# Raw FFN weights loaded ahead of the second batch's v, one weight conversion moved into the attention, and named places for x and the last h

## The chip, the core and the metric

The kernel runs on one core of one Trainium2 chip. A core has a matrix engine (TensorE, in the rows PE, with its weight loads as PEld), three elementwise engines (VectorE as DVE, ScalarE as ACT, GpSimd as POOL) and a sync engine (SP) that here issues nearly all transfers. Each engine works its own list of instructions in order; semaphores join them. The metric is the device time of one execution in microseconds.

## The reference

What is computed, cut to what matters here:

```python
# attention, B=2, H=8, S=576, D=64: two parts that are added
#  q, k and v averaged over groups of 4 -> softmax attention on 144 positions, repeated 4 times
#  plus attention in which a position sees only those less than 4 away
x = attn_out                                  # 1152 tokens x 512
h = x @ w_in; g = relu(h) + log1p(exp(-|h|))  # w_in 512 x 2048
x = g @ w_out                                 # w_out 2048 x 512
P = exp(x @ w_gate - max)                     # 8 experts, then 8 rounds of row and column norms
out = sum over e of P[:, e] * (relu(x @ w1[e]) @ w2[e])
```

The FFN's weights come as 64-bit floats and the answer is wanted in 32-bit accuracy.

## The kernel before

There are three stages, and the order of every engine's list is fixed before the run by a scheduler that follows the order of the code, the waits and a timeline of its own.

**Attention** (to about 121 us). `emit` walks 36 units: 16 pooled ones (`pooled`, tiles named with a d: pd, ptd, pvd, pxd) and 20 local ones (`local`, with an l: pl, ptl, pvl, pxl), batch 0 first. A unit has four steps on PE: scores (pd or pl), transposes (pt), values (pv), and a transpose back (px). Step k of a unit is written two units behind step k-1, so four units are under way at once. DVE takes the maximum (nm) and normalises, ACT does the exponentials (e) and copies the transposes (ptls, ptds, upT), DVE adds both parts into xf, and GpSimd splits xf into a rounded part and the rest in x. There are three x tiles of 384 tokens, x0 to x2. `fill` and `warm` add products of zeros.

The v of batch 1 for the pooled part comes by `load_vd(1)`: two transfers vr of 640 KB, which GpSimd adds up into vs and then vd. Its vs tiles use the same buffers (tags "ch" and "cs", one of each) as the weight conversion below. The local part's v comes by small transfers vw.

**FFN** (to about 305 us). Four blocks of 512 of the 2048 middle columns, for each three chunks of 384 tokens: `l1` (products ph, line 471, then softplus on ACT and DVE into h) and `l2` (products py, line 513, added into yp). Each block needs four weight tiles of two halves, made by `prep(n)`, n = 0 to 15: `load_raw` brings 1 MB of 64-bit numbers (raw, two buffers), and `from_double` turns them into w with three ACT and seven DVE instructions (lines 133 to 146; in the first four the last of the seven runs on GpSimd). `prep(n)` also loads raw n+2. The first block's conversions and its first products are placed among the attention units by the table `at`; `prep(4)` and all later ones are called in the FFN loop, after the first, second or third `l1` of a block.

**Experts** (to the end). Products pu (line 564) and po (line 613) with weights prepared from 32-bit numbers.

The SP queue holds its transfers in the order of the code: k and q of batch 1, then vr twice, then raw 0 and raw 1, then vw, and further raw between the vw. A transfer whose buffer is not free stops all behind it.

Places: the three x tiles, the two vr tiles of batch 1 and later s0 shared a pool of three turning buffers (`xyp`, tag "xy"). The last h of the FFN had a pool of its own (`late`). The weight tiles turn over six places, four in `wp` and two in `wp2`, and `wp2` is opened only when the attention's pools are closed.

Of the kernel before, what the change touches and what calls it, by code (L numbers as in the profile page):

```python
# [8 lines left out]
F32 = mybir.dt.float32  # L9
F32R = mybir.dt.float32r  # L10
# [11 lines left out]
P = 128  # L22
# [10 lines left out]
CH = 384  # L33
NCH = NT // CH
KD = DM // P
FB = 512
NFT = FB // P
NFB = FF // FB
# [5 lines left out]
WIN = [min(max(HQ * t - POOLF + 1, 0), S - KW) for t in range(2 * NQT)]  # L44
OFF = [tuple(HQ * t - WIN[t] for t in (2 * u, 2 * u + 1)) for u in range(NQT)]
KINDS = sorted(set(OFF))
NRING = 6
EARLY = 4
PAIR = CH // 2
# [31 lines left out]
class Net:  # L81
# [66 lines left out]
    def prep(self, n):  # L148
        if n >= 4 * NFB:
            return  # L150
        self.load_raw(n)
        i = n % NRING
        pool = self.wp if i < EARLY else self.wp2
        w = pool.tile([P, 2, 1024], F32R, tag=f"w{i}", name=f"w{n}")
        self.from_double(n, w)
        self.load_raw(n + 2)
        self.ws[n] = w
# [128 lines left out]
    def load_vd(self, b):  # L286
        nc = self.nc
        vd = self.atp.tile([GH, 2, H, DA], F32, tag="vd", name=f"vd{b}", bufs=2)
        nc.gpsimd.memset(vd[:, :, :, D:DA], 1.0)
        for hf in range(2):  # L290
            pool, tag = (self.rawp, "raw") if b == 0 else (self.xyp, "xy")
            r = pool.tile([GP, POOLF, DM], F32, tag=tag, name=f"vr{b}{hf}")
            nc.sync.dma_start(out=r, in_=self.a["vp"][b, hf].rearrange("p (f d) -> p f d", f=POOLF))
            s = self.convp.tile([GH, 2, DM], F32, tag=("ch", "cs")[hf], name=f"vs{b}{hf}", bufs=1)
            e = nc.vector if b == 0 else nc.gpsimd
            e.tensor_tensor(s, r[:GH, 0:2], r[:GH, 2:4], ALU.add)
            sv = s.rearrange("p f (h d) -> p f h d", h=H)
            e.tensor_tensor(vd[:, hf, :, 0:D], sv[:, 0], sv[:, 1], ALU.add)
        self.vd[b] = vd
        self.upT[b] = self.atp.tile([P, NPAIR, G], F32, tag="upT", name=f"upT{b}", bufs=2)  # L300
# [65 lines left out]
    def local(self, b, t, g):  # L366
# [56 lines left out]
        def s4():  # L423
# [16 lines left out]
            while n < nq:  # L440
                c, o = divmod(tok + n, CH)
                m = min(nq - n, CH - o)
                if c not in self.x:
                    self.x[c] = self.xyp.tile([P, 2, KD, CH], F32R, tag="xy", name=f"x{c}")
                hi, lo = (self.x[c][:, i, 2 * g : 2 * g + 2, o : o + m] for i in range(2))
                nc.gpsimd.tensor_copy(hi, xf[:, :, n : n + m])
                nc.gpsimd.tensor_tensor(lo, xf[:, :, n : n + m], split(hi), ALU.subtract)
                n += m
# [44 lines left out]
        self.made = (act.ins, dve.ins)  # L493

    def l1(self, blk, c, nf=2):
        pool, tag = (self.late, "h") if (blk, c) == (NFB - 1, NCH - 1) else (self.hp, "h")
        h = pool.tile([P, 2, NFT, CH], F32R, tag=tag, name=f"h{blk}_{c}")
        self.h[blk, c] = h
        return [lambda f=f: self.l1_unit(blk, c, f, nf, h) for f in range(0, NFT, nf)]
# [242 lines left out]
    def run(self):  # L742
        stack = ExitStack()
        xstack = ExitStack()
        self.xyp = xstack.enter_context(self.tc.tile_pool(name="xyp", bufs=NCH))
        self.attention_pools(stack)
        self.h, self.ypart, self.acc, self.wa, self.T = {}, {}, {}, {}, {}
        self.x = {}
# [46 lines left out]
                self.load_qk(1, p)  # L795

        def load_rest():
            self.load_vd(1)
            self.load_raw(1)

        def prep(n, lag):

# [6 lines left out]
        at = {1: [load_second], 9: [load_rest]}  # L809
        for p in range(NPAIR):  # L810
            at.setdefault(11 + p, []).append(lambda p=p: self.pool_qk(1, p))
        for n, lag, u in zip(range(2 * NFT), (1, 1, 0, 0), (16, 19, 23, 29)):
            at.setdefault(u, []).append(lambda n=n, lag=lag: prep(n, lag))
        one, two, after = self.l1(0, 0, 1), self.l2(0, 0, 1), self.l1(0, 1, 1)
        for m, u in zip(one + two[:2], (22, 24, 26, 28, 30, 32)):
            at.setdefault(u, []).append(m)
        at[36] = [after[0], after[1], two[2], after[2], after[3], two[3]]
# [15 lines left out]
        def opened(name, to=self.ctx, **kw):  # L833
            return to.enter_context(self.tc.tile_pool(name=name, reuse_waits="tile", **kw))

        def edge(name, to=self.ctx):
            opened(name, to, bufs=1, side="right").tile([P, EDGE], F32, name=name)
# [34 lines left out]
        for b, c in items[: -NCH + 1]:  # L872
            first_product(b, c)
            if c == 1:
                self.prep(4 * (b + 1) + 1)
            if c == 2:
                self.prep(4 * (b + 1) + 2)
            if pending not in (None, (0, 0)):
                second_product(*pending)
            if c == 0:  # L880
                self.prep(4 * (b + 1))
            if c == 2:
                self.prep(4 * (b + 1) + 3)
            pending = (b, c)

        b = NFB - 1
        wstack.close()
        self.ap = opened("ap", bufs=1, side="right")
        edge("edge2")
        self.late = opened("late", bufs=1, side="right")  # L890

        s0 = self.xyp.tile([P, 2, 4, 2, P], F32, tag="xy", name="s0")
        parts = [(0, i, *part) for i in range(2) for part in self.sums_up(0, i, s0[:, i])]
        first_product(b, 1)
        first_product(b, 2)
        turn_over()
        for n in (1, 3, 0):
            self.behind(lambda: self.part_up(*parts[n]))
        second_product(b, 0)
# [128 lines left out]
```

## Time and profile before

| | us |
|---|---|
| runs of the kernel before, median of 3 | 1057.45 |
| lowest and highest of them | 1054.2 and 1062.04 |
| the profiled execution, its own time | 1064.65 |
| span of the profiled execution | 1062.9 |
| instructions | 16399 |

The span is what the trace shows between the first and the last instruction; the profiled execution's own time is 1.75 us more. The profile lists for each engine what it did and what it waited for, and for PE the clock that the chip granted it: 1.00 is its upper level, 2.4 GHz, and 0.50 its lower, 1.2 GHz. PE is counted busy for 1050.3 of the 1062.9 us, but a product at the lower clock counts as busy too, for longer.

### The profile page before, as it was taken

What the parts mean: (1) busy time and instruction counts of PE and PEld (TensorE: products, weight loads), DVE (VectorE), ACT (ScalarE), POOL (GpSimd) and SP (SyncE); (2) the same over time, 40 slices, a digit from 0 to 9 for tenths busy, and PEclk for the clock granted to TensorE, in tenths of its full rate; (3) what the DMA queues carried; (4) which work ended last, traced back from release to release, by engine and by line L of the source; (5) the groups of instructions that cost most, each with busy time, mean ns of one, the idle gap of its engine ahead of it and who ended that gap; (6) DMA issues with size and microseconds to landing.
All of it is one profiled execution on the core that took longest, in us unless ns stands there. A gap on an engine that the chain in (4) does not pass through costs nothing.

```text
span 1062.9 us, 16399 instructions
## 1 busy us (share of the span) xinstructions
PE 1050.3 (99%) x6570; PEld 945.1 (89%) x6570; DVE 775.2 (73%) x1470; ACT 428.7 (40%) x815; POOL 162.5 (15%) x210
## 2 busy tenths in 40 slices
PE   8999999999999999999999999999999999999998
PEld 5667999999998899898989989898998989899897
DVE  6578699999987687784947658494765848576572
ACT  5567697776743433241413324141331414133130
POOL 2653300002112220111202011120201112020000
PEclk9789999999999999999999999999999999999999
DMA  9532032222111221111211111121111112110003
GB/s 286 167 97 75 2 119 80 80 80 80 40 40 40 80 80 40 40 41 40 80 40 41 40 40 40 40 81 40 40 40 41 41 40 80 41 40 1 1 2 89
DMA packets 14348, 63.92 MB, mean 60 GB/s; under 512 B 1792, under 2 KB 4608, under 8 KB 7808
## 3 DMA queue, kind: packets, MB, share of 16 engines
q1 hardware_dynamic: 13696, 61.70, 17.9%
q8 instruction: 51, 0.84, 0.3%
q10 hardware_dynamic: 576, 1.18, 0.3%
q14 instruction: 25, 0.20, 0.1%
HBM read 60.51 MB, written 2.36 MB: 59 GB/s over the span
## 4 chain that ended last, share of the span: by engine, by line
PE 89%; DVE 5%; DMA 3%; ACT 2%; issue 1%; SPq 0%; DVEq 0%; ACTq 0%
PE po L613 37%; PE pu L564 33%; PE ph L471 7%; PE py L513 6%; DMA raw<-in_w 1%; DMA k<-in_k 1%; PE pvl L406 1%; PE pl L385 1%; DMA vw<-in_vw 1%; DVE h L492 1%; PE pxl L426 1%; DVE r L488 1%; DVE l L489 1%; DVE yp L525 0%; PE pd L320 0%
## 5 line engine op out<-in xcount | busy, mean ns | idle before, releaser
L564 PE MATMUL pu<-T,a 128*128 128x320 f32 (+1 forms) x2688 | 354.6, 293 | 1.4 <-DVE yp L525 1.4
L564 PEld LDWEIGHTS pu<-T,a 128*128 128x128 f32 x2688 | 351.7, 188 | 3.0 <-issue 1.7
L613 PE MATMUL po<-w,h 128*128 128x512 f32 x960 | 221.3, 390 | 0.0
L635 DVE SCALAR_TENSOR_TENSOR acc<-po,prob,acc 128x512 f32<-128x512 f32 x126 | 94.1, 748 | 173.6 <-PE po L613 173.6
L613 PEld LDWEIGHTS po<-w,h 128*128 128x128 f32 x960 | 179.9, 188 | 37.3
L197 ACT CAST w<-raw 128x1024 fp32r<-128x1024 f32 x32 | 33.4, 1052 | 271.4 <-PE po L613 271.4
L613 PE MATMUL po<-w,h0a 128*128 128x512 f32 x576 | 142.3, 390 | 0.5 <-DVE w L198 0.5
L166 POOL TENSOR_TENSOR s<-raw 128x256 f32<-128x256 f32 x32 | 28.6, 892 | 677.9 <-DVE a L177 472.8
L613 PEld LDWEIGHTS po<-w,h0a 128*128 128x128 f32 x576 | 107.3, 188 | 22.4 <-DVE w L198 0.9
L513 PE MATMUL py<-h,w 128*128 128x384 f32 x576 | 104.0, 336 | 0.6 <-DVE l L490 0.3
L471 PE MATMUL ph<-x,w 128*128 128x384 f32 x576 | 104.4, 336 | 0.0
L513 PEld LDWEIGHTS py<-h,w 128*128 128x128 f32 x576 | 99.7, 188 | 1.7 <-DVE h L492 0.8
L471 PEld LDWEIGHTS ph<-x,w 128*128 128x128 f32 x576 | 99.7, 188 | 0.6 <-issue 0.4
L576 ACT ACTIVATE h<-c 128x320 fp32r<-128x320 f32 x128 | 58.6, 468 | 80.2 <-DVE c L587 80.2
L577 DVE SCALAR_TENSOR_TENSOR h<-c,h 128x320 fp32r<-128x320 f32 x128 | 67.9, 539 | 0.3
L587 DVE TENSOR_TENSOR c<-v,pu 128x256 f32<-128x256 f32 (+1 forms) x128 | 57.6, 450 | 10.9 <-PE pu L564 7.9
L576 ACT ACTIVATE h0a<-c 128x256 fp32r<-128x256 f32 x96 | 37.5, 417 | 50.3 <-DVE c L587 50.0
L198 DVE TENSOR_TENSOR w<-raw,w 128x1024 fp32r<-128x1024 f32 x32 | 39.0, 1219 | 22.1 <-ACT w L197 22.1
L613 PE MATMUL po<-w,h0b 128*128 128x512 f32 x192 | 54.3, 389 | 0.0
L613 PEld LDWEIGHTS po<-w,h0b 128*128 128x128 f32 x192 | 36.0, 188 | 7.5
L585 ACT COPY p<-pu 128x256 f32<-128x256 f32 (+1 forms) x64 | 25.2, 393 | 36.8 <-PE pu L564 35.1
L577 DVE SCALAR_TENSOR_TENSOR h0a<-c,h0a 128x256 fp32r<-128x256 f32 x96 | 39.0, 419 | 0.8 <-ACT h0a L576 0.5
(139 smaller groups left out, 1207.8 us busy)
## 6 DMA issues: line engine op xcount, KB each, us to landing
raw<-in_w SPq DMA_DIRECT2D x48, 1024.0 KB, 4.9
vw<-in_vw SPq DMA_DIRECT2D x20, 130.0 KB, 4.1
vr<-in_vp SPq DMA_DIRECT2D x4, 640.0 KB, 10.3
k<-in_k SPq DMA_DIRECT2D x8, 288.0 KB, 6.6
out<-acc SPq DMA_DIRECT2D x5, 256.0 KB, 2.0
q<-in_q ACTq DMA_DIRECT2D x4, 288.0 KB, 5.9
q<-in_q SPq DMA_DIRECT2D x4, 288.0 KB, 7.1
out<-acc SPq DMA_DIRECT2D x8, 128.0 KB, 2.3
```

The lines of the kernel that those rows point to most:

```text
L166: nc.gpsimd.tensor_tensor(s[:, 0], a21, a22, ALU.add)
L197: nc.scalar.copy(w[:, 0], raw)
L198: nc.vector.tensor_tensor(w[:, 1], raw, split(w[:, 0]), ALU.subtract)
L471: nc.tensor.matmul(ps[:, i], lhsT=wv[:, a, k, fo : fo + P], rhs=x[:, b, k], start=(n == 0), stop=(n == 3 * KD - 1),)
L513: nc.tensor.matmul(ps[:, a], lhsT=w[:, i, d * P : (d + 1) * P], rhs=h[:, j, f], start=(n == 0), stop=(n == 3 * NFT - 1),)
L564: nc.tensor.matmul(ps, lhsT=w[:, x, a, k], rhs=t[:, y, b, k], start=(m == 0), stop=(m == 5))
L576: act = nc.scalar.activation(hi, src, AF.Relu)
L577: dve = nc.vector.scalar_tensor_tensor(lo, src, 0.0, split(hi), ALU.max, ALU.subtract)
L585: nc.scalar.copy(to, ps)
L587: nc.vector.tensor_tensor(to, src, ps, ALU.add)
L613: nc.tensor.matmul(ps, lhsT=self.h[s, i, f][:, at * P : (at + 1) * P], rhs=w[:, j], start=(n == 0), stop=(n == 3 * NFT - 1),)
L635: nc.vector.scalar_tensor_tensor(acc, ps, pe, acc, ALU.mult, ALU.add)
```

## The change

Four things change in the code.

- `load_rest` issues raw 0 and raw 1 before the two vr of batch 1, not behind them.
- `prep(4)`, the first conversion of the FFN's second block, is called at unit 34 of the attention and no longer in the FFN loop. Its w tile has a new pool `wp4`, which is there from the start. In its wake each later conversion of the FFN stands where the one before it stood, and the last block is without one.
- The three turning buffers of `xyp` get names: x0 is always in "xc", x1 in "xb", x2 in "xa", and the two vr of batch 1 in "xa" and "xb".
- The last h has x1's place, "xb", and the pool `late` is opened later, when x is done with, for an expert tile only.

```diff
@@ prep
-        pool = self.wp if i < EARLY else self.wp2
+        pool = self.wp if i < EARLY else self.wp4 if i == EARLY else self.wp2
@@ load_vd
-            pool, tag = (self.rawp, "raw") if b == 0 else (self.xyp, "xy")
+            pool, tag = (self.rawp, "raw") if b == 0 else (self.xyp, "xa" if hf == 0 else "xb")
@@ local, s4   (PLACE = ("xc", "xb", "xa"))
-                    self.x[c] = self.xyp.tile([P, 2, KD, CH], F32R, tag="xy", name=f"x{c}")
+                    self.x[c] = self.xyp.tile([P, 2, KD, CH], F32R, tag=PLACE[c], name=f"x{c}")
@@ l1
-        pool, tag = (self.late, "h") if (blk, c) == (NFB - 1, NCH - 1) else (self.hp, "h")
+        pool, tag = (self.xyp, PLACE[1]) if (blk, c) == (NFB - 1, NCH - 1) else (self.hp, "h")
@@ run
+        self.wp4 = xstack.enter_context(self.tc.tile_pool(name="wp4", bufs=1))
-        self.xyp = xstack.enter_context(self.tc.tile_pool(name="xyp", bufs=NCH))
+        self.xyp = xstack.enter_context(self.tc.tile_pool(name="xyp", bufs=1))
@@ load_rest
+            self.load_raw(1)
             self.load_vd(1)
-            self.load_raw(1)
@@ run, the table at
+        at[34] = [lambda: prep(4, 0)]
@@ run, the FFN loop
-            if c == 0:
+            if c == 0 and b > 0:
                 self.prep(4 * (b + 1))
@@ run, after the loop: edge("edge2") and the pool late move behind turn_over()
```

The first place is the SP queue, the list of transfers, from the end of batch 1's k and q on. Before:

```order
L293 DMA vr_476<-in_vp 80x2048
L293 DMA vr_481<-in_vp 80x2048
L117 DMA raw_487<-in_w 128x2048
L117 DMA raw_489<-in_w 128x2048
L283 DMA vw_116<-in_vw 64x2x260 x2
L283 DMA vw_117<-in_vw 64x2x260 x2
L117 DMA raw_809<-in_w 128x2048
L283 DMA vw_118<-in_vw 64x2x260 x2
L117 DMA raw_941<-in_w 128x2048
L283 DMA vw_116<-in_vw 64x2x260 x2
```

And now (line numbers are up by one; raw_477 and raw_479 are raw 0 and 1, raw_812 and raw_944 raw 2 and 3):

```order
L118 DMA raw_477<-in_w 128x2048
L118 DMA raw_479<-in_w 128x2048
L294 DMA vr_483<-in_vp 80x2048
L294 DMA vr_488<-in_vp 80x2048
L284 DMA vw_119<-in_vw 64x2x260 x2
L284 DMA vw_120<-in_vw 64x2x260 x2
L118 DMA raw_812<-in_w 128x2048
L284 DMA vw_121<-in_vw 64x2x260 x2
L284 DMA vw_119<-in_vw 64x2x260 x2
L118 DMA raw_944<-in_w 128x2048
```

The two raw have passed the two vr, and raw 3 now stands behind one more pair of vw.

The second place is ACT's list around the first conversion, which reads raw 0: its first ACT instruction writes cm (line 135 before, 136 now), its second cs (133 before, 134 now). Before:

```order
L399 COPY ptls<-ptl 128x256
L309 ACTIVATE e<-pl,nm 128x64 x4
L337 COPY ptds<-ptd 72x288
L135 ACTIVATE cm<-raw_487 128x1024
L362 COPY upT_194<-pxd 128x72
L309 ACTIVATE e<-pd,nm 72x144 x2
L399 COPY ptls<-ptl 128x256
L267 ACTIVATE kd_660<-kd_660 128x144
L309 ACTIVATE e<-pl,nm 128x64 x4
L267 ACTIVATE kd_708<-kd_708 128x144
L337 COPY ptds<-ptd 72x288
L133 ACTIVATE cs<-raw_487 128x1024
```

And now, the stretch from two rows ahead of the same upT copy on:

```order
L310 ACTIVATE e<-pd,nm 72x144 x2
L136 ACTIVATE cm<-raw_477 128x1024
L363 COPY upT_197<-pxd 128x72
L400 COPY ptls<-ptl 128x256
L310 ACTIVATE e<-pl,nm 128x64 x4
L268 ACTIVATE kd_663<-kd_663 128x144
L338 COPY ptds<-ptd 72x288
L268 ACTIVATE kd_711<-kd_711 128x144
L363 COPY upT_197<-pxd 128x72
L310 ACTIVATE e<-pd,nm 72x144 x2
L400 COPY ptls<-ptl 128x256
L310 ACTIVATE e<-pl,nm 128x64 x4
```

The cm instruction has moved up past a ptds copy, a set of four local exponentials (e<-pl), a ptls copy and an upT copy. The cs instruction has moved the other way: where one set of local exponentials lay between the two, five do now (the last three are behind the rows shown).

The third place is DVE's list among the last attention units, from the xf at which the moved conversion begins. Before:

```order
L433 TENSOR_TENSOR xf<-pxl,upT_486 128x232
L420 TENSOR_TENSOR ull<-pvl,rrl 128x256
L306 TENSOR_REDUCE nm<-pl 128x4
L352 TENSOR_SCALAR rsd<-pvd 72x2
L354 RECIPROCAL rrd<-rsd 72x2
L356 TENSOR_TENSOR uld<-pvd,rrd 72x128
L306 TENSOR_REDUCE nm<-pl 128x4
L416 TENSOR_SCALAR rsl<-pvl 128x4
L418 RECIPROCAL rrl<-rsl 128x4
L433 TENSOR_TENSOR xf<-pxl,upT_486 128x232
```

And now:

```order
L434 TENSOR_TENSOR xf<-pxl,upT_493 128x232
L137 TENSOR_SCALAR cm<-cm 128x1024
L421 TENSOR_TENSOR ull<-pvl,rrl 128x256
L307 TENSOR_REDUCE nm<-pl 128x4
L139 TENSOR_SCALAR cm<-cm 128x1024
L353 TENSOR_SCALAR rsd<-pvd 72x2
L307 TENSOR_REDUCE nm<-pl 128x4
L140 SCALAR_TENSOR_TENSOR ch<-raw_1140,cm 128x1024
L355 RECIPROCAL rrd<-rsd 72x2
L417 TENSOR_SCALAR rsl<-pvl 128x4
L434 TENSOR_TENSOR xf<-pxl,upT_493 128x232
L143 TENSOR_SCALAR ca<-raw_1140 128x1024
```

Four of the conversion's seven DVE instructions (raw_1140 is raw 4) now stand between the small ones of the attention here; the other three follow within the next eight.

## Rows read from the trace of the kernel before

**Rows 1.** The page's first line.
```profile
span 1062.9 us, 16399 instructions
```

**Rows 2.** Windows: stretch, length, each engine's busy time, clock, DMA; columns first.
```profile
core 0: us, PE busy (x) PEld busy (x) DVE busy (x) ACT busy (x) POOL busy (x), PEclk, DMA share, GB/s
38.90:58.97 20.07, 20.07 (x142) 13.25 (x141) 12.46 (x31) 10.78 (x34) 10.56 (x9) 0.50 0.21 68
60.00:70.00 10.00, 10.00 (x102) 6.52 (x100) 7.73 (x25) 7.86 (x22) 7.35 (x9) 1.00 0.53 159
90.00:100.00 10.00, 10.00 (x114) 8.08 (x113) 9.77 (x24) 8.14 (x25) 4.81 (x3) 1.00 0.38 120
100.00:120.00 20.00, 19.98 (x185) 16.45 (x186) 12.74 (x42) 11.53 (x37) 5.64 (x15) 1.00 0.03 9
128.00:232.00 104.00, 104.00 (x601) 104.00 (x601) 100.51 (x120) 78.15 (x94) 0.06 (x1) 1.00 0.25 82
232.00:306.00 74.00, 72.02 (x414) 71.12 (x414) 72.18 (x86) 48.74 (x60) 10.12 (x10) 1.00 0.16 57
306.00:1062.00 756.00, 751.84 (x4482) 682.04 (x4480) 512.15 (x1026) 222.18 (x428) 94.81 (x121) 1.00 0.14 46
```

**Rows 3.** Timeline of ACT: start, length, operation, count [idle before, releaser].
```profile
29.84 0.24 ACT L362 COPY upT<-pxd 128x72 f32<-128x72 f32 x1
...
32.99 0.40 ACT L337 COPY ptds<-ptd 72x288 f32<-72x288 f32 x1 [1.24 <-PE ptd L335]
36.77 1.13 ACT L135 ACTIVATE cm<-raw 128x1024 f32<-128x1024 f32 x1 [3.39 <-DMA raw<-in_w]
37.81 0.19 ACT L362 COPY upT<-pxd 128x72 f32<-128x72 f32 x1
...
78.36 1.14 ACT L135 ACTIVATE cm<-raw 128x1024 f32<-128x1024 f32 x1
```

**Rows 4.** Timeline of PE over the stall and the units behind it.
```profile
35.10 0.66 PE L406 MATMUL pvl<-vw,ptls 128*64 128x130 f32 x8
38.06 0.44 PE L426 MATMUL pxl<-perm,ull 128*128 128x128 f32 x2 [2.29 <-ACT upT L362]
38.60 0.37 PE L374 MATMUL pl<-mask,identb 128*128 128x256 bf16 x1
...
58.66 0.42 PE L374 MATMUL pl<-mask,identb 128*128 128x256 bf16 x1
...
66.01 0.27 PE L374 MATMUL pl<-mask,identb 128*128 128x256 bf16 x1
```

**Rows 5.** Timeline of GpSimd: batch 1's v, and two casts of one shape.
```profile
31.25 2.35 POOL L296 TENSOR_TENSOR vs<-vr 72x1024 f32<-72x1024 f32 x1 [3.75 <-DMA vr<-in_vp]
34.11 2.34 POOL L296 TENSOR_TENSOR vs<-vr 72x1024 f32<-72x1024 f32 x1 [0.52 <-DMA vr<-in_vp]
...
38.40 0.38 POOL L446 CAST x<-xf 128x232 fp32r<-128x232 f32 x1
38.73 1.27 POOL L298 TENSOR_TENSOR vd<-vs 72x512 f32<-72x512 f32 x1
...
62.57 2.33 POOL L446 CAST x<-xf 128x232 fp32r<-128x232 f32 x1 [4.69 <-DVE xf L433]
```

**Rows 6.** Timeline of the SP queue: raw 3 and the vw behind it.
```profile
61.93 0.33 SPq L117 DMA_DIRECT2D raw<-in_w  x1
63.49 7.78 SPq L283 DMA_DIRECT2D vw<-in_vw  x4
```

**Rows 7.** Groups by line, 128 to 305 us: the conversion's longest instructions (mean ns).
```profile
L139 DVE SCALAR_TENSOR_TENSOR ch<-raw,cm 128x1024 int32<-128x1024 int32 x12 | 15.2, 1263 | 0.1
L138 DVE TENSOR_SCALAR cm<-cm 128x1024 int32<-128x1024 int32 x12 | 8.6, 718 | 0.1
L133 ACT ACTIVATE cs<-raw 128x1024 f32<-128x1024 uint32 x12 | 13.8, 1150 | 4.0 <-DVE w L146 4.0
```

**Rows 8.** PE's waits, 120 to 345 us: total us, times, longest.
```profile
PE pu L564 <- DVE yp L525: 1.4, 1, 1.4
```

More of the change, by code (lines that the diff above doesn't have):

```diff
@@ L46 @@
 KINDS = sorted(set(OFF))
+PLACE = ("xc", "xb", "xa")
 NRING = 6
@@ L888, in run @@
         self.ap = opened("ap", bufs=1, side="right")
-        edge("edge2")
-        self.late = opened("late", bufs=1, side="right")
-        s0 = self.xyp.tile([P, 2, 4, 2, P], F32, tag="xy", name="s0")
+        s0 = self.xyp.tile([P, 2, 4, 2, P], F32, tag=PLACE[0], name="s0")
         parts = [(0, i, *part) for i in range(2) for part in self.sums_up(0, i, s0[:, i])]
@@ L896, in run @@
         turn_over()
+        edge("edge2")
+        self.late = opened("late", bufs=1, side="right")
         for n in (1, 3, 0):
```

## The prediction

> **What bounds the kernel now.** I read the windows first, then the timelines at the places where PE stands still or slow. From 128 us on PE is the bound and has hardly a hole: 104.00 busy of 104 us, then 72.02 of 74, then 751.84 of 756 [rows 2]. The order of that last part is not touched, so what the change can move lies before 306 us: the attention (to about 121 us), and the 1.98 us that PE loses between 232 and 306 us.
>
> In the attention one stall stands out. ACT reached the first conversion's cm instruction after 32.99 + 0.40 = 33.39 us and waited 3.39 us for raw 0 [rows 3], with the small copies and exponentials queued behind it. PE went on until 35.10 + 0.66 = 35.76 and then stood 2.29 us, released by the upT copy behind cm [rows 4]. From 38.90 to 58.97 us PE's granted clock is then 0.50, its lower level of 1.2 GHz, and PE is busy for all 20.07 us [rows 2]; by 60 us it is 1.00 again. So the late raw 0 costs twice: the stall, and five units at the lower clock. Their price: from the scores product at 38.60 to the one at 58.66 are five units in 20.06 us, and from 58.66 to 66.01 three units in 7.35 us, 2.45 each [rows 4]. Five at that pace are 12.25 us, so the lower clock cost 20.06 - 12.25 = 7.81 us.
>
> **The sum's base.** The trace is of an execution of 1064.65 us (span 1062.9, [rows 1], and 1.75 around it), 7.2 above the median of the runs, 1057.45. Take off stall and slow clock, 2.29 + 7.81 = 10.10, and 1054.55 is left, which is near the fastest run, 1054.2. I read the runs, 1054.2 to 1062.04, as executions in which the clock fell for a shorter time or not at all. No row of theirs shows it, so it stays a reading; but by it the change saves some 10 us against the profiled execution and only 2 or 3 against the median.
>
> **Raw 0 ahead of vr.** The queue works in order. The two vr landed at 31.25 and 34.11 [rows 5] and raw 0 at 36.77 [rows 3]: 2.86 us for a vr, 2.66 for a raw, back to back. What was ahead of them was thus done at 31.25 - 2.86 = 28.39. With raw first, raw 0 lands at 31.05, raw 1 at 33.7, the vr at 36.6 and 39.4. But the order now puts cm ahead of the upT copy that ran at 29.84 [rows 3]. ACT so waits about 31.05 - 29.84 = 1.2 us and is held, with cm's 1.13, for 2.34 us. Before, it was held from 33.39 to 37.90, 4.51 us, of which PE went on for 2.37 and lost 2.29. By the same cover the new hold costs PE about nothing; the ends are 0 and 2.34. I take 0.2, as the hold is as long as the cover: -2.29 + 0.2 = **-2.1**.
>
> **The clock.** With a pause of 0.2 us in place of 2.29 I expect it to stay at 1.00: **-7.8**. Ends: 0 if it falls all the same, and -10.0 if all 20.07 us halve. I take the measured pace because in 60 to 70 us, at the full clock, DVE (7.73 of 10), ACT (7.86) and GpSimd (7.35) had room left with PE dense [rows 2].
>
> **Batch 1's v, later.** GpSimd now starts its two sums at 36.6 and 39.4, each 2.35, is through at 41.75, and after one cast (0.38) and two vd of 1.27 at 44.7, against 38.73 + 1.27 = 40.0 before [rows 5]. The vd themselves are wanted only by batch 1's units. But vs shares its buffers with the conversion: cs cannot be written before the second vd is done. In the new order cs stands behind the fifth set of local exponentials after cm. Those of 30.81 us being the first, the fifth come about five units later, 30.81 + 5 x 2.45 = 43.1, and are done by 44.0. ACT so waits some 0.7 us, and DVE, at ch, about as long. Ends: 0, as a hold of 0.7 + 1.15 is shorter than the cover of 2.37, and 2.3, if the holds of both engines show. I take **+0.7**, a third of the way.
>
> **Prep(4) among the last units.** Seven DVE instructions come in, four of at most 0.72 us and three of at most 1.26, 6.7 us, and three on ACT of at most 1.15, 3.5 us [rows 7]. They go where DVE was busy 12.74 of 20 us and ACT 11.53 [rows 2], so DVE comes to 19.4 of 20. At 90 to 100 us DVE was busy 9.77 of 10 and PE lost nothing [rows 2]. Ends: 0 and 6.7, each delayed microsecond reaching PE. I take **+0.5**, near the lower end by that row. Casts of the same shape took GpSimd 0.38 and 2.33 us in the attention [rows 5], so something can hold it up there. The Trainium skill (SBUF — State Buffer, "SBUF: two separate sides") says why and speaks against this edit: a DVE instruction with two SBUF inputs and a GpSimd instruction that reads SBUF lock each other out for the whole instruction. By that rule three of the seven would hold up GpSimd, and with it x, by up to 3 x 1.26 = 3.8 us, and this term would be 3.8 and not 0.5. Since GpSimd was busy for only 5.64 of these 20 us [rows 2], I keep 0.5.
>
> **The last FFN block.** Every later conversion moves up by one place and the last block has one fewer: 6.7 us less for a DVE that was busy 72.18 of 74 us there. PE lost 1.98 us [rows 2], of which 1.4 was the wait for the last addition to yp, ahead of the first expert product [rows 8]. That addition cannot begin before PE's last FFN product ends, so most of that wait stays. The other 0.6 I take as gained, and 0.4 of the 1.4: **-1.0**. Ends 0 and -2.0.
>
> **Edits at nothing.** Raw 3 was issued at 61.93, and behind the further vw it cannot go before 63.49 [rows 6]; at 5 us to land that is 68.4 by the old clock, and its conversion began at 78.36 [rows 3]: ten us of cover. The named places: the last h is first written after PE's products with x1, which stand ahead on PE, and w4's pool is free from the start. If that cover were gone, it would be a wait of one chunk's products behind the last l1, and PE would show it.
>
> **The sum.** -2.1 - 7.8 + 0.7 + 0.5 - 1.0 = -9.7, and 1064.65 - 9.7 = 1054.95: **1055 us**, 0.2% below the median.
>
> **The rivals.**
> 1. *The clock falls all the same*, at the hold near 31 us or at the one near 44: 1055 + 7.8 = 1062.8, a little less if it falls late. For it: two holds in place of one, and a kernel whose clock gave way to 2.29 us. Against it: each hold is about the cover or shorter. If this is so the change does not do what it says, and all it leaves is the last block's microsecond.
> 2. *DVE becomes the bound among the last units*: 19.4 of 20 us is full, and xf and nm wait behind 1.26 us pieces. All of 6.7 reaching PE in place of 0.5: 1055 + 6.2 = 1061. Against it: the 90 to 100 us row.
> 3. *Slower: GpSimd's backlog stops the FFN's first products.* The 4.7 us by which vd is late sit in front of the casts that fill x0, and l1's first products need x0 and the w that GpSimd makes. If PE stands there for all 4.7 us and the clock falls again (7.8), it is 1055 + 12.5 = 1067.5, slower than before. It decides, against the median, once the pause and the slow clock together come to 1057.45 - 1055 = 2.5 us. Against it: GpSimd was busy 10.56 of 20.07 us there [rows 2], so at the faster pace it has 12.25 for about 10.6.
> 4. *More than I count*: all 10.0 for the clock, 2.29, and 2.0 in the last block, nothing lost: 1064.65 - 14.3 = 1050.4.
>
> **How the numbers follow.** The forecast 0.58, rival 1 0.20, rival 2 0.12, rival 3 0.06, rival 4 0.04. The predicted time is the forecast's. The range goes from rival 4's 1050.5 to 1062.5, which takes in rival 2 and the half of rival 1 in which the clock falls late; left out are rival 3, the other half of rival 1 and what lies under 1050.5, less than 0.2. The likeliest case's own range is 1052 to 1058, on both sides of the median. One per cent, 10.6 us, is about what a measurement of this kernel can tell from no change. Faster by more would need less than 1046.9, beyond rival 4: 0.04. Slower by more would need 1068, rival 3 and a little: 0.05. Within: 0.91.
>
> **What would show it.** In the new profile: granted clock 1.00 from 30 to 70 us; ACT's wait for raw at 1 to 1.5 us and none of over 1 us on PE behind it; the second vd done near 45; the unit pace 2.45 us; the last attention unit and the first dense FFN product some 9 us earlier; PE's loss in the last block about 1 us. The prediction is wrong if the clock is at 0.50 anywhere behind 30 us, if PE waits for xf, x or w between 45 and 120 us for more than a microsecond in sum, or if the runs lie outside the range with none of this.

## The result

| | before | after |
|---|---|---|
| median of 15 runs each, us | 1062.04 | 1065.83 |
| lowest and highest, us | 1054.2 and 1064.85 | 1062.7 and 1071.26 |
| ratio after to before | | 1.0055, 95% interval 1.0034 to 1.0076 |
| profiled execution, us | 1064.65 | 1071.26 |
| its mean granted clock | 0.990 | 0.986 |

The changed kernel is 0.55% slower, where 0.2% faster was forecast. It is within one per cent, but above the top of the range, 1062.5. Part of that is the base: the three runs I was shown had a median of 1057.45, these fifteen 1062.04.

**Profile after.** The page's first line and windows of the stretches that matter, with PE's, DVE's and GpSimd's busy time and the granted clock in the places that the first line names. They answer [rows 1, 2].

```profile
span 1069.5 us, 16400 instructions
```

```profile
core 0: us, PE busy (x) PEld busy (x) DVE busy (x) ACT busy (x) POOL busy (x), PEclk, DMA share, GB/s
...
35.00:40.00 5.00, 3.17 (x51) 2.50 (x52) 4.88 (x4) 0.81 (x4) 4.71 (x3) 1.00 0.15 35
40.00:45.00 5.00, 4.12 (x35) 2.75 (x35) 4.85 (x14) 2.25 (x10) 4.68 (x6) 0.72 0.20 47
...
80.00:90.00 10.00, 8.45 (x56) 6.70 (x55) 7.27 (x19) 6.07 (x20) 3.96 (x3) 0.66 0.17 51
...
100.00:110.00 10.00, 8.19 (x65) 6.86 (x65) 6.31 (x18) 4.61 (x15) 4.90 (x7) 0.68 0.14 36
...
232.00:320.00 88.00, 87.70 (x528) 87.36 (x527) 81.56 (x102) 52.21 (x68) 13.04 (x10) 1.00 0.14 49
```

From 35 to 40 us DVE is busy for 4.88 us with only four instructions and GpSimd for 4.71 with three, while PE idles. From there to 60 us the clock is mostly at 0.50, and it falls twice more, in 80 to 90 and in 100 to 110 us; worked out from all windows, PE ran some 30 us at the lower level, against 20 before [rows 2]. The last FFN block is the one good sign: 0.30 us lost in 88.

The instructions behind it, in time order on ACT, DVE and GpSimd (start, length, operation, count, idle time before and its releaser). They answer [rows 3, 5].

```profile
28.62 1.17 ACT L136 ACTIVATE cm<-raw 128x1024 f32<-128x1024 f32 x1
...
41.25 0.93 ACT L310 ACTIVATE e<-pl,nm 128x64 f32<-128x64 f32 x4 [4.18 <-DVE nm L307]
```

```profile
35.77 4.72 DVE L137 TENSOR_SCALAR cm<-cm 128x1024 f32<-128x1024 f32 x1
40.41 0.41 DVE L421 TENSOR_TENSOR ull<-pvl,rrl 128x256 f32<-128x256 f32 x1
```

```profile
35.29 4.65 POOL L297 TENSOR_TENSOR vs<-vr 72x1024 f32<-72x1024 f32 x2 [1.94 <-DMA vr<-in_vp]
39.88 0.84 POOL L447 CAST x<-xf 128x232 fp32r<-128x232 f32 x1
40.69 2.94 POOL L299 TENSOR_TENSOR vd<-vs 72x512 f32<-72x512 f32 x2
```

ACT's wait for raw 0 is gone. In its place DVE's first cm, one of sixteen with a median of 0.69 us, took 4.72. It began 0.48 us after GpSimd began its two sums vs, and it ended 0.55 us after they did. It waited for no semaphore; it was simply long. Behind it in DVE's list stood ull and nm, behind nm ACT's exponentials, and behind ull PE.

PE's three longest pauses in the attention (a fourth, of 1.04 us, ends at 120.33), and its first expert product. They answer [rows 4, 8].

```profile
37.48 0.68 PE L386 MATMUL pl<-k,q 64*64 64x64 f32 x16
40.88 0.38 PE L221 MATMUL ptl<-z 128*128 128x512 bf16 x1 [2.71 <-DVE ull L421]
...
81.88 0.44 PE L336 MATMUL ptd<-ident,e 72*72 72x72 f32 x4 [1.55 <-DVE uld L357]
...
101.86 0.25 PE L362 MATMUL pxd<-ident,uld 72*128 72x72 f32 x1 [1.81 <-DVE uld L357]
...
312.04 6.17 PE L565 MATMUL pu<-T,a 128*128 128x256 f32 x51
```

The pauses at 81.88 and 101.86 have the same sign. Ahead of each, DVE's r (line 489; others of these 128x384 ones take 0.54 us) was long while GpSimd made a w:

```profile
79.60 2.02 DVE L489 SCALAR_TENSOR_TENSOR r<-r,e 128x384 f32<-128x384 f32 x1
```

```profile
78.84 2.37 POOL L147 TENSOR_TENSOR w<-cs,ch 128x1024 fp32r<-128x1024 f32 x1 [5.22 <-DVE ch L145]
```

The r began at 79.60, the w ended at 81.21, and r ended 0.41 us later. At 98.90 it is 2.62 us beside the next w. So the theory to test was: while GpSimd sums or multiplies, certain DVE instructions stand still, and the new load order puts the two sums on the conversion. The first expert product begins 6.62 us later than before (305.42), and the trace ends 6.6 us later; all of the loss lies in the attention.

**Pause and clock apart.** Each run has its span's mean clock, and within one kernel the time follows it: over 280 runs of the fifteen kernels of this study that were timed often enough (before and after among them), a mean clock lower by 0.010 costs 8.4 us. (Worked out by [rows 2], it is about the same: 20.07 us at 0.50 lower the mean of 1062.9 us by 0.0094, which by this slope is 7.9 us, and I had read 7.81 from the units.) One run of vs_dve, 1143.23 us at a mean clock of 0.851, is left out of all this. With that slope a kernel's mean time splits into its time at clock 1.000 and what the lower clock adds. In seven of these kernels, after and swap_only among them, no run stood at 1.000, so that column is extrapolated there:

| kernel | ratio to before, 95% interval | mean clock | at 1.000, us | clock adds, us |
|---|---|---|---|---|
| before (116 runs) | | 0.9956 | 1055.3 | 3.7 |
| after | 1.0055, 1.0034 to 1.0076 | 0.9914 | 1059.0 | 7.2 |
| swap_only | 1.0081, 1.0054 to 1.0109 | 0.9900 | 1060.4 | 8.4 |
| prep4_only | 0.9985, 0.9963 to 1.0007 | 0.9958 | 1053.9 | 3.6 |
| vs_dve | 1.0002, 0.9982 to 1.0023 | 0.9935 | 1054.4 | 5.4 |
| w_dve | 1.0006, 0.9986 to 1.0026 | 0.9962 | 1056.7 | 3.2 |
| both_dve | 1.0022, 1.0003 to 1.0042 | 0.9953 | 1059.1 | 3.9 |
| p4_w | 1.0040, 1.0016 to 1.0064 | 0.9942 | 1058.9 | 4.8 |
| prep0_later | 1.0006, 0.9987 to 1.0025 | 0.9965 | 1057.1 | 2.9 |
| p4_late | 1.0018, 0.9999 to 1.0036 | 0.9952 | 1057.9 | 4.1 |
| p4_17 | 1.0048, 1.0026 to 1.0070 | 0.9932 | 1058.4 | 5.7 |
| fill_pause | 0.9972, 0.9952 to 0.9993 | 0.9991 | 1056.1 | 0.8 |
| fillpin | 1.0016, 0.9994 to 1.0037 | 0.9972 | 1057.9 | 2.4 |
| before_fill | 1.0028, 1.0006 to 1.0051 | 0.9957 | 1057.1 | 3.6 |
| p4_fill | 1.0024, 0.9997 to 1.0051 | 0.9958 | 1058.1 | 3.6 |

So 3.7 us of the change's loss are pauses and work, and 2 to 3.5 the clock (the fifteen runs of before that stand beside those of after had a mean of 1060.45 us, all 116 of 1059.1).

### The profile page after: what moved, and what is told of

It is laid out like the page before. It is cut to its first block, busy times and chain, and to the rows that moved or that the text cites. A ratio compares the mean times of both kernels' runs of the same rounds, so it can differ in the third digit from the quotient of the medians.

```text
span 1069.5 us, 16400 instructions
## 1 busy us (share of the span) xinstructions
PE 1054.0 (99%) x6570; PEld 949.4 (89%) x6570; DVE 783.0 (73%) x1470; ACT 429.4 (40%) x815; POOL 168.3 (16%) x210
## 3 DMA queue, kind: packets, MB, share of 16 engines
q10 hardware_dynamic: 576, 1.18, 0.3%
## 4 chain that ended last, share of the span: by engine, by line
PE 92%; DVE 5%; DMA 2%; ACT 1%; issue 1%; POOL 0%; SPq 0%; DVEq 0%
PE po L614 37%; PE pu L565 32%; PE ph L472 8%; PE py L514 8%; PE pvl L407 1%; DMA k<-in_k 1%; PE pl L386 1%; DVE r L489 1%; DMA vr<-in_vp 1%; PE pxl L427 1%; DVE cm L137 1%; PE pd L321 1%; PE ptl L398 0%; PE pvd L345 0%; PE ptl L221 0%
## 5 line engine op out<-in xcount | busy, mean ns | idle before, releaser
L577 ACT ACTIVATE h0a<-c 128x256 fp32r<-128x256 f32 x96 | 37.5, 417 | 50.5 <-DVE c L588 50.1
```

Source lines behind the costliest of these rows:

```text
L577: act = nc.scalar.activation(hi, src, AF.Relu)
```

## The experiments

**1. Which of the two edits.** swap_only is the kernel before with the new load order alone; prep4_only is the changed kernel with the order undone.

```diff
 def load_rest():
-    self.load_vd(1)
     self.load_raw(1)
+    self.load_vd(1)
```

> The kernel before with one edit: raw 0 and raw 1 issued ahead of batch 1's vr; prep(4) stays in the FFN loop. Theory (lock): the late vs sums on GpSimd hold DVE's first cm instruction, PE stands about 2.7 us near 41 us and the clock falls behind it; the attention is longer by some 5 us and the FFN gains nothing, so about 1067 us, ratio 1.005 to 1.008, and cm takes 4 to 5 us. Rival (DVE load): the slowdown comes from prep(4) among the last units, so this edit alone gives the gain that was forecast for it, 1055 to 1060, ratio 0.995 to 1.000.

> The changed kernel with the order of the loads undone: vr ahead of raw again, prep(4) at unit 34 and the named places kept. Theory (lock): raw 0 is late again as in the kernel before (ACT waits about 3.4 us, PE 2.3), no 4.7 us cm, and the last FFN block gains its 2 us: ratio 0.997 to 1.000. Rival (DVE load): the seven instructions among the last units cost what the changed kernel lost, ratio 1.004 to 1.008.

The waits of PE over a microsecond in the attention, 20 to 137 us (total, times, longest), in swap_only, with its first cm, and then in prep4_only:

```profile
PE pxd L361 <- DVE uld L356: 1.8, 1, 1.8
PE ptd L335 <- DVE uld L356: 1.5, 1, 1.5
PE pvl L220 <- DVE uld L356: 1.5, 1, 1.5
```

```profile
35.76 2.61 DVE L136 TENSOR_SCALAR cm<-cm 128x1024 f32<-128x1024 f32 x1
```

```profile
PE pxl L427 <- ACT upT L363: 1.3, 1, 1.3
PE pxd L362 <- DVE uld L357: 1.2, 1, 1.2
```

The order alone is slower than the whole change, the rest alone is at or under the kernel before. In swap_only the ratio came out at the upper end of what the theory had, but not in its way: cm was held for 2.61 us and not for 4 to 5, and in place of one pause of 2.7 us near 41 there are three of 1.5 to 1.8 later on. At clock 1.000 the order costs 1059.0 - 1053.9 = 5.1 us with prep(4). Without it the difference is the same, 1060.4 - 1055.3 = 5.1, but that the two agree is chance: 1.9 us of the second are two pauses of 1.3 and 0.6 us in the FFN, which swap_only has and the other three kernels have not (experiment 2 shows where they come from), and 3.2 are left. With the old order prep(4) and the named places bring 1055.3 - 1053.9 = 1.4 us. The loss is the order's.

**2. Is it GpSimd's work?** vs_dve puts batch 1's sums vs and vd on DVE, w_dve the last multiplication of the first four conversions; both_dve does both. p4_w is w_dve with the old load order.

```diff
-            e = nc.vector if b == 0 else nc.gpsimd       # load_vd
+            e = nc.vector
...
-        e = nc.gpsimd if n < NFT else nc.vector          # from_double
+        e = nc.vector
```

> The changed kernel with batch 1's vs and vd sums on DVE in place of GpSimd (3.8 us more for DVE, 7.2 us less for GpSimd). Theory (lock): the first cm is back at 0.7 us, the pause of 2.7 us near 41 us is gone or below 1 us, and the clock's first fall with it: 3 to 7 us faster than the changed kernel, ratio to before 0.999 to 1.003. Rival (DVE load): DVE has more to do, nothing improves: ratio 1.005 or more.

> The changed kernel with the last multiplication of the first four conversions on DVE in place of GpSimd (4.9 us more for DVE, 9.4 us less for GpSimd). Theory (lock): the later pauses, 1.55 us at 82 and 1.81 us at 102, in which a DVE instruction of 0.54 us took 2.0 and 2.6 us beside that multiplication, are gone with their two falls of the clock; the first one at 41 stays: 2 to 6 us faster than the changed kernel, ratio to before 1.000 to 1.004. Rival (DVE load): ratio 1.006 or more.

> Two edits on the changed kernel: batch 1's four v sums and the last multiplication of the first four conversions go from GpSimd to DVE. Theory (a GpSimd instruction that reads SBUF holds up certain DVE instructions, and the new load order puts the two on top of each other): both holds go, the 4.72 us cm takes under 1 us, the r instructions at 2.0 and 2.6 us fall to some 0.55, PE has no pause over 1.5 us before 120 us, and the median is below those of the two single edits (1059.9 and 1059.7): 1056 to 1058. Rival (the loss is DVE's load, which this edit raises by some 4 x 1.2 + 4 x 1.2 = 9.6 us): above both single edits, 1061 or more.

> The changed kernel with the old load order (v ahead of raw 0), and with the last multiplication of the first four conversions on DVE. Theory: the order, not prep(4) or the named places, is what loses; with the order undone the first cm no longer meets the v sums (0.7 to 1.6 us), and without w on GpSimd the r instructions are not held either: 1054 to 1057, at or under the 1056.8 of the kernel with the old order alone. Rival (DVE has no room for 4 x 1.2 us more): 1058 to 1061.

DVE's first cm in vs_dve, and then cm and an r in w_dve:

```profile
38.23 0.68 DVE L137 TENSOR_SCALAR cm<-cm 128x1024 f32<-128x1024 f32 x1
```

```profile
35.67 4.50 DVE L137 TENSOR_SCALAR cm<-cm 128x1024 f32<-128x1024 f32 x1
...
76.32 0.56 DVE L489 SCALAR_TENSOR_TENSOR r<-r,e 128x384 f32<-128x384 f32 x1
```

Each edit takes away just the hold that belongs to it, though both give DVE, the busier engine, more to do: with the sums on DVE cm takes 0.68 us, with w on DVE cm is still held for 4.50 and r is not. Each alone brings the ratio from 1.0055 to about 1. So DVE's load is not what loses in the changed kernel. One thing expected of vs_dve did not come: PE still has pauses of 1.45 and 1.39 us near 40 us, behind ACT's e and DVE's rrl, and the clock of its profiled execution fell there all the same.

The two together I had wrong. both_dve was to come under either and came out above both, and p4_w lost 5.0 us at clock 1.000 against prep4_only. The rival's point, that DVE has no room for them, may be part of that; no run shows it by itself. Another part is not DVE's load at all. Both kernels have a pause of 1.3 us at the FFN's second block and one of 0.6 later, 1.9 us that after, w_dve, vs_dve and prep4_only don't have, and so have seven of the other kernels. Kernels fillpin (below) and w_dve are alike on PE to some 0.02 us from 105 to 130.00 us, and then (PE and ACT of fillpin, ACT of w_dve):

```profile
139.78 2.55 PE L472 MATMUL ph<-x,w 128*128 128x384 f32 x13 [1.29 <-ACT yp L524]
```

```profile
137.16 1.16 ACT L136 ACTIVATE cm<-raw 128x1024 f32<-128x1024 f32 x1
138.19 0.86 ACT L486 ACTIVATE r<-e 128x768 f32<-128x768 f32 x1
138.92 0.81 ACT L524 COPY yp<-py 128x768 f32<-128x768 f32 x1
```

```profile
136.15 0.80 ACT L524 COPY yp<-py 128x768 f32<-128x768 f32 x1
```

In one list ACT's copy out of py, for which PE waits, stands ahead of r, in the other behind cm and r. The scheduler orders each list anew after any edit, so a comparison of two of these kernels holds to about 2 us only where their lists agree. What else p4_w lost is open.

**3. Without moving work to another engine.** prep0_later is the changed kernel with `prep(0)` two units later (and `prep(1)` one): cm then meets the sums no more. p4_late is the same with the old load order, p4_17 with `prep(0)` at 17.

```diff
-        for n, lag, u in zip(range(2 * NFT), (1, 1, 0, 0), (16, 19, 23, 29)):
+        for n, lag, u in zip(range(2 * NFT), (1, 1, 0, 0), (18, 20, 23, 29)):
```

> The changed kernel with prep(0) two units later and prep(1) one unit later; no work changes its engine, and the loads keep the new order. Theory: the first cm then runs near 41 us, behind the v sums (which end at 39.9), and takes 0.7 to 1.6 us in place of 4.72; PE's pause of 2.7 us at 40.9 goes, and with it part of the clock's fall: 1059 to 1063, as the later holds by w stay. Rival (the new order loses because batch 1's v and so GpSimd's casts come later): the pause and the time stay at 1065 to 1067, or grow, since w0 also comes 5 us later.

> The changed kernel with the old load order (v ahead of raw 0) and with prep(0) two units later and prep(1) one: the same prep edit that was run with the new order, so that the two edits can be crossed. Raw 0 lands near 36.8 us as before, and the conversion now asks for it after that. Theory: no wait for raw 0, the v sums are over when cm comes (the two vd, to 40, may hold it to some 2 us), PE has no pause over 1.3 us before 60 us, and the clock stays up in most runs: 0.995 to 0.998 of before, 1053 to 1057. Rival (w0 two units later stops the first FFN products, as the 2.9 us wait for x did with the new order): 1.000 to 1.003.

> As the kernel before, but prep(0) only one unit later than in the changed kernel (prep(1) one unit later too), old load order. Theory: the conversion asks for raw 0 some 2.4 us later than before, so of the wait of 3.4 us one of about 1 us is left, under the cover that PE has; cm falls behind the v sums, beside the two vd: 0.995 to 0.999 of before. Rival (what matters is w0's lateness for the first FFN products): between the kernel with the old order alone (0.9985) and the one with prep(0) two units later.

DVE and GpSimd in prep0_later:

```profile
40.27 2.85 DVE L137 TENSOR_SCALAR cm<-cm 128x1024 f32<-128x1024 f32 x1
```

```profile
40.09 2.48 POOL L299 TENSOR_TENSOR vd<-vs 72x512 f32<-72x512 f32 x2
42.53 0.83 POOL L447 CAST x<-xf 128x232 fp32r<-128x232 f32 x1
```

The time came out as the theory had it (1060.59 us, ratio 1.0006), the cm did not: it ran into the two vd and was held for 2.85 us. It ended 0.55 us after them, as it had ended 0.55 us after vs, and the cast behind them took 0.83 where such casts take 0.38 [rows 5]: GpSimd waits in its turn. Crossed with p4_late, the order that cost 5.1 us with prep(0) at 16 costs 1057.1 - 1057.9 = -0.8 us with prep(0) at 18. So the new order is not bad in itself; it is bad where the sums meet a conversion. Both kernels lose time elsewhere: PE waits 2.9 us for x in prep0_later and 2.5 in p4_late, where it is 0.7 in the changed kernel. p4_late and p4_17 both miss. The scheduler left ACT's cm as early in its list as ever, so ACT waited 2.83 and 4.16 us for raw 0, and PE 1.7 and 3.1 us behind it: a later call does not by itself move every instruction of a step.

**4. The hold by itself.** vs_twice does each vs sum twice; probe runs six forms of DVE instruction beside two GpSimd sums of vs' shape, ahead of everything else.

```diff
-            e.tensor_tensor(s, r[:GH, 0:2], r[:GH, 2:4], ALU.add)
+            for _ in range(1 + b):
+                e.tensor_tensor(s, r[:GH, 0:2], r[:GH, 2:4], ALU.add)
```

> The changed kernel with each of batch 1's two vs sums done twice over on GpSimd (the same result twice): four instructions of 2.34 us in place of two, 35.3 to 44.7 us. Theory: the first cm on DVE, which took 4.72 us, is held until they end: 8.5 to 9.5 us, and PE's pause behind it grows from 2.7 to 7 or more. Rival (cm is slow because of the loads landing in SBUF at that time, or because of its own buffers): cm stays at 4.7 us, and only what needs vs (vd, ch, cs) comes later.

> The changed kernel with some 40 us of extra work ahead of everything, on tiles of its own: six DVE forms, each run once beside two vs-shaped GpSimd sums (72x1024, 2.34 us each) and once alone. Its time says nothing, only these rows do. Theory (the hold is between the engines, not in this kernel's data): the tensor_scalar of cm's form, 0.69 us alone, takes up to 4.7 us beside the sums, its int32 form and the two forms with two SBUF inputs (1.2 us alone) likewise wait for a sum's end; the two forms that read PSUM run at their own length. Rival (cm was slow because of loads that landed meanwhile): all six take the same time beside the sums as alone, within 20%.

vs_twice, DVE and GpSimd:

```profile
35.91 4.59 DVE L137 TENSOR_SCALAR cm<-cm 128x1024 f32<-128x1024 f32 x1
...
41.09 2.51 DVE L139 TENSOR_SCALAR cm<-cm 128x1024 int32<-128x1024 int32 x1
```

```profile
35.30 4.65 POOL L298 TENSOR_TENSOR vs<-vr 72x1024 f32<-72x1024 f32 x2 [1.81 <-DMA vr<-in_vp]
39.90 0.84 POOL L448 CAST x<-xf 128x232 fp32r<-128x232 f32 x1
40.70 5.11 POOL L298 TENSOR_TENSOR vs<-vr 72x1024 f32<-72x1024 f32 x2
```

cm did not grow to 8.5 us: the scheduler put a cast between the two pairs, and there cm got its turn. The second pair held the next instruction, the int32 tensor_scalar (0.69 us else), for 2.51. The prediction of size fell; that the hold follows GpSimd's work, it shows.

The probe's forms on DVE, each twice (line 222 an int32 tensor_scalar, shown with its shortest, median and longest; 224 with two SBUF inputs, 225 with one input in PSUM), then GpSimd ahead of line 222's and around line 224's, and a window around the latter, with the DMA share as the last number but one:

```profile
L222 DVE TENSOR_SCALAR ta<-ta x2: 917/1885/2853, 14.6 to 15.5; 128x1024 int32<-128x1024 int32 x2
```

```profile
25.56 6.75 DVE L224 TENSOR_TENSOR tb<-ta,tb 128x1024 f32<-128x1024 f32 x2
...
32.54 1.42 DVE L225 TENSOR_TENSOR tb<-pq,ta 128x512 f32<-128x512 f32 x2
```

```profile
12.09 2.84 POOL L231 TENSOR_TENSOR ps<-pr 72x1024 f32<-72x1024 f32 x1 [1.61 <-DVE tok L234]
...
25.48 2.33 POOL L231 TENSOR_TENSOR ps<-pr 72x1024 f32<-72x1024 f32 x1 [1.23 <-DVE tok L232]
27.77 1.18 POOL L229 COPY tok<-tok 128x1 f32<-128x1 f32 x1
28.90 2.33 POOL L231 TENSOR_TENSOR ps<-pr 72x1024 f32<-72x1024 f32 x1
```

```profile
24.50:32.50 8.00, 0.00 (x0) 0.00 (x0) 7.93 (x9) 0.00 (x0) 5.79 (x4) 1.00 0.00 0
```

The scheduler put both copies of a form beside a sum, so "alone" comes from the kernel's own rows. The forms with two SBUF inputs (lines 223 and 224) took 3.38 us each, against 1.26 [rows 7] and 1.22 in the kernel before: the first of line 224 stood from 25.56 to the end of the sum at 25.48 + 2.33 = 27.81, and then ran about its own length. Of the two int32 tensor_scalars one took 0.92 and the other, beside the sum of 15.48, 2.85, against 0.72. The two forms that read PSUM (lines 225 and 226), on half as many columns, took 0.71 each beside a sum and held nothing. Nor is every form held whose input is in SBUF: the kernel's own tensor_reduce of q took 0.73 us beside the sum of 12.09 and 0.73 to 0.74 alone. The other way round, GpSimd's copy of one column, 0.18 us else, took 1.18 behind a two-input form. cm's own form missed its sums: one copy ran between two of them, the other began at 12.05, just ahead of the sum of 12.09, and this sum took 2.84 us. Loads are not what holds: the kernel's own still land until about 24 us (DMA share 0.98 from 12 to 24 us), and cm's form took 0.67 us among them, while line 224 was held with no load at all. The hold lies between the two engines. The Trainium skill (SBUF — State Buffer, "Who interferes with whom") gives it as a lock on a pair of ports that the two engines share, taken by whichever starts first for a whole instruction, by DVE's copies and tensor_scalar in their faster modes as well as by its instructions with two SBUF inputs. These rows agree for the two-input forms and the int32 tensor_scalar, and the changed kernel's own 4.72 us for cm's form.

**5. What the clock has in it.** Four kernels add twelve products of zeros on PE. fill_pause was to put them into PE's pause behind cm.

```diff
                         u[k]()
                         n += 1
+                        if k == 0 and self.begun == 15:
+                            self.warm(12)
```

> The changed kernel with twelve further products on zeros (results unused) on PE between the scores product at 37.5 us and the transpose at 40.9, where PE stood 2.71 us behind the held cm. The DVE hold stays. Theory (the pause makes the clock fall): without an idle PE there the long stretch at half clock (17 us in the profiled run) does not come in most runs, the mean clock rises from 0.991 to some 0.995, and the ratio to before falls from 1.0055 to 1.002 or 1.003. Rival (the clock falls with the work that follows, or with the later pauses alone): clock and ratio stay, or the ratio grows by the products that outlast the pause, up to 2 us.

They stood too early: the scheduler spread them over 28 to 34 us, and GpSimd's list changed with them. DVE and GpSimd there:

```profile
38.48 0.69 DVE L137 TENSOR_SCALAR cm<-cm 128x1024 f32<-128x1024 f32 x1
```

```profile
35.57 2.36 POOL L297 TENSOR_TENSOR vs<-vr 72x1024 f32<-72x1024 f32 x1 [1.65 <-PE pvd L345]
...
38.25 0.37 POOL L447 CAST x<-xf 128x232 fp32r<-128x232 f32 x1
38.59 2.80 POOL L297 TENSOR_TENSOR vs<-vr 72x1024 f32<-72x1024 f32 x1
```

The sums came apart, cm ran between them at its own 0.69 us, and now the second sum was the longer one. No pause of over 1.2 us is left, eleven of twelve runs have a clock of 0.998 or more, the other 0.995. With 0.9972 (0.9952 to 0.9993) this is the one kernel here that is faster than the kernel before beyond its interval, and it is faster than the changed one too. But it says nothing of a pause with PE kept busy, so three more were run.

fillpin pins the products behind the scores product at 37.5 us (`with self.tc.issue_after(self.pe.ins)` around them), with DVE's and GpSimd's order there unchanged, though cm, expected at 4.7 us, was held for 2.32; before_fill and p4_fill put fill_pause's early ones into the kernel before and into prep4_only.

> The changed kernel with twelve products on zeros on PE exactly between the scores product at 37.5 us and the transpose that waits for the held cm (behind that scores product in PE's order); the order of DVE and GpSimd up to there and past cm is as in the changed kernel. cm so stays held for some 4.7 us. Theory (PE's pause brings the clock down): PE is busy through the pause, the long half-clock stretch behind it does not come in most runs, the mean clock of the runs rises from 0.991 to 0.995 or more, and the ratio falls from 1.0055 to 1.001 to 1.003; the 2.7 us of the hold itself stay. Rival (the clock falls with what follows, whatever PE did): clock near 0.991 and ratio 1.005 to 1.007.

> The kernel before with the twelve early filling products (three, six and three of them between the products of the units at about 28 to 34 us). Nothing of the change is in it. Theory (the products only delay PE by their own 2.6 us, which the late raw 0 then costs less): the pause of 2.29 us shrinks or goes, the clock stays up in more runs: 0.996 to 0.999. Rival (the gain of the same products in the changed kernel, 0.9972, came from parting the v sums from cm, which in the kernel before do not meet): 1.000 to 1.002.

> The changed kernel with the old load order and the same twelve early filling products. At clock 1.000 the kernel with the old order alone took some 1054 us, and its median of 1056.8 has some 3.5 us of lower clock in it. Theory: the products take up the 1.3 us pause behind raw 0, the clock stays at 1.000 in most runs, and the time is 1054 to 1055.5, 0.995 to 0.997 of before, under both kernels. Rival (another interleaving of the later units costs what it saves, as with w on DVE and the later prep(0)): 0.999 to 1.003.

In fillpin PE's products fill the place of the pause:

```profile
38.49 2.76 PE L214 MATMUL pz<-z 128*128 128x512 bf16 x12
```

Its time at clock 1.000 is 1057.9, near the changed kernel's 1059.0, but that is not a like sum: the products take 2.76 us, ACT's late copy 1.9, and the later pauses of the attention are shorter (1.2 us at most), since the lists behind 60 us are other ones. The lower clock adds 2.4 us in place of 7.2, and the ratio is 1.0016. How much of these 4.8 us is the filled pause's and how much the later ones', fillpin cannot say. w_dve can say something, for it keeps the first pause and has no other over 1.03 us (PE, and the windows around the pause, the clock as the last number but two):

```profile
40.56 0.38 PE L221 MATMUL ptl<-z 128*128 128x512 bf16 x1 [2.49 <-DVE ull L421]
```

```profile
35.00:40.00 5.00, 3.07 (x51) 2.40 (x51) 4.91 (x4) 0.70 (x3) 5.00 (x3) 1.00 0.17 34
40.00:45.00 5.00, 4.44 (x61) 3.21 (x60) 4.93 (x14) 3.28 (x15) 4.68 (x6) 1.00 0.19 53
```

The clock stayed at 1.00 behind this pause, in that execution to the end, and over the runs of w_dve the lower clock adds 3.2 us. So a pause of 2.5 us need not bring the clock down, and the later pauses have a large part in the changed kernel's 7.2: without them (w_dve) it is 4.0 us less, without the held cm (vs_dve) 1.8 less, each with lists of its own. That PE standing still is what costs clock fits fillpin and fill_pause, but before_fill, whose longest pause is 1.1 us, still loses 3.6. What each pause costs is not shown.

before_fill and p4_fill gain nothing (1.0028, 1.0024): where no sums meet a conversion, the same products cost 1.8 and 4.2 us at clock 1.000 (1.9 of the latter by ACT's other order). So it is not the products that made fill_pause faster. Its cm and sums are parted, and its later pauses are 1.2 us at most; the two are not told apart.

## Why the prediction was wrong

- **The base and the reading of the runs: right.** Runs of the kernel before differ by how long the clock was low; at 1.000 they take 1055.3 us, where I had worked out 1054.55.
- **Raw 0 ahead of vr: right.** cm started at 28.62 us without a wait. The loads came earlier than I had them (raw 0 by 28.62, for 31.05; second vr before 37.6, for 39.4; second vd done at 43.6, for 44.7).
- **Batch 1's v, later: the step that failed.** I counted what waits for vs' data and buffers, +0.7 us. cm waits for neither, and was held for 4.72 - 0.69 = 4.0 us by the sums being at work; PE lost 2.71. Two r were held in the same way by w, and PE lost 1.55 and 1.81 there, for which the sum had no term. I had the rule in hand, and in the prediction applied it only to prep(4)'s three instructions with two SBUF inputs. I did not ask which DVE instructions would stand beside the moved sums, nor whether tensor_scalar is among the forms that are held. The trace of before had the row: cm's shortest, median and longest,

```profile
L136 DVE TENSOR_SCALAR cm<-cm x16: 680/685/1634, 38.9 to 261.5; 128x1024 f32<-128x1024 f32 x16
```

  and the one of 1.63 us lies at 38.92, beside the vd of 38.73 [rows 5].
- **The clock: wrong, and behind pauses that this step left out.** I expected -7.8 us, as no pause was left. A new one of 2.71 us came where the old one of 2.29 had been, and behind it two of 1.55 and 1.81; in the profiled execution about 30 us ran at 0.50, not 0. Rival 1 had the clock fall "all the same", but through the two holds of ACT, which PE did not feel. That the clock follows from the size of a pause, as I took it, the runs bear out only in part: behind w_dve's pause of 2.49 us the clock of the profiled execution did not fall.
- **Prep(4) among the last units: right.** +0.5 was forecast. prep4_only against the kernel before gives prep(4) and the places -1.4 in all at clock 1.000, of which the last block is -1.7, so +0.3; in the trace PE has one new wait there, of 1.2 us. GpSimd's lock was no 3.8 us here.
- **The last FFN block: right in direction.** 0.30 us lost of 88 where 1.98 were of 74: the gain is 1.7 us, near the end of my bounds, 2.0. yp's wait ahead of the first expert product went whole. But the scheduler can give it back: the kernels with ACT's late copy lose 1.9 us in the blocks ahead of it.
- **Edits at nothing: right.** No wait for raw 3, the named places or w4 shows in PE's waits.
- **The rivals.** Rival 3 had nearly the size (1067.5) but not the mechanism: PE waited for x only once, 0.69 us. I gave it 0.06. None of the four had a DVE instruction that grows without waiting.
- **The sum, put right at clock 1.000:** between the traces PE's idle time from 20 to 130 us grows from 3.1 to 8.0 us, +4.9, and the last block gives -1.7, together +3.2, where the forecast's terms without the clock came to -1.9; the split of the runs has +3.7. The other half microsecond is open.

## What to carry to other kernels

When a GpSimd instruction that reads SBUF moves in time, list the DVE instructions that will run beside it, and price those with two SBUF inputs, and a tensor_scalar of this size from SBUF to SBUF, as held until the GpSimd work ends; no wait in the profile names this, only a length above that instruction's own median. Where PE is the bound, such a hold can cost twice, once as a pause and again through the granted clock, and the second price differs from run to run. And judge a change of order with the whole new lists in view: an edit here reordered ACT a hundred microseconds later, for 1.9 us.

## What the runs showed that I had not expected

- A hold can outlast one instruction: cm stood behind two sums back to back (4.72, 4.59 and 4.50 us in three kernels), but in fillpin and swap_only the same cm was let in between them (2.32 and 2.61 us) and the pair took 5.1 in place of 4.65. What decides that is open.
- The hold goes both ways: GpSimd's 0.18 us copy took 1.18 behind a DVE form with two SBUF inputs.
- A mean clock lower by 0.010 costs this kernel 8.4 us. With a pause of 2.7 us filled with products of no use and the later pauses shorter, the low clock took 2.4 us in place of 7.2; with the pause left and the later ones shorter, 3.2.
